# Two-block FFN groups with paired biases and a new order of issue in a sliding-window attention and highway FFN kernel

## The chip, the cores and the metric

The kernel runs on one core of one Trainium2 chip. The metric is the time of one execution on the device in microseconds (us). Before the change it is 175.66 us, the median of three runs (175.21 to 183.57). Executions fall into a fast and a slow state; in the slow one the granted clock of TensorE is mostly lower (0.961 in the slow run of the changed kernel, 0.971 to 0.982 in its fast ones).

Engines: PE is TensorE, PEld its weight loads, DVE is VectorE, ACT is ScalarE, POOL is GpSimd, SP is SyncE, which issues the stores.

## The reference, cut to what matters

```python
# attention: B = H = 8, S = 576, D = 64; a window of 128 keys, ALiBi bias
scores = scale * np.matmul(q, k.transpose(0, 1, 3, 2))
mask = (rel >= 0) & (rel < window)
scores = np.where(mask, scores + bias[None], -1000000000.0)
attn = softmax(scores)                    # written out in the original
x = attn @ v                              # rearranged to 4608 tokens x 512
# highway FFN
H = np.maximum(x @ w_h, 0.0)
T = 1.0 / (1.0 + np.exp(-(x @ w_t + b_t)))
out = T * H + (1.0 - T) * x
```

## The kernel before

Two batches go through the kernel as a pair, so there are four pairs. For each: GpSimd issues the loads (which cast to bf16), TensorE transposes Q and K, and computes scores; ScalarE takes the exponential, VectorE multiplies by the mask, TensorE multiplies by V, VectorE normalises into x. The FFN then works on blocks of 128 tokens, 36 in all:

```python
def f_h(m, kind, gi, i):                       # TensorE: H = x w_h, one PSUM bank
    AH[m, kind, gi] = ps_tile(1)
    for c in range(NCK):                       # NCK = 4
        nc.tensor.matmul(out=AH[m, kind, gi], lhsT=XT[m, kind, gi][:, i, c, :],
                         rhs=wH[:, c, :], start=c == 0, stop=c == NCK - 1)

def f_u(m, kind, gi):                          # VectorE: u = relu(H) - x
    ...
def f_z(m, kind, gi, i):                       # TensorE: Z = x w_t, then + b_t by a fifth matmul
    AZ[m, kind, gi] = ps_tile(1)
    az = AZ[m, kind, gi]
    for c in range(NCK):
        nc.tensor.matmul(out=az, lhsT=XT[m, kind, gi][:, i, c, :], rhs=wT[:, c, :],
                         start=c == 0, stop=False)
    nc.tensor.matmul(out=az, lhsT=ones1[:], rhs=bT[:], start=False, stop=True)

def f_th(m, kind, gi):                         # ScalarE: tanh(Z/2), float16
    ...
def f_t(m, kind, gi, eng):                     # GpSimd mostly: T = 0.5 tanh + 0.5
    tt = TT[m, kind, gi][:, 0 : grp(m, kind, gi)[1], :]
    eng.tensor_scalar(out=tt, in0=tt, scalar1=0.5, scalar2=0.5, op0=ALU.mult, op1=ALU.add)

def f_g(m, kind, gi):                          # VectorE: u = u T
    ...
def f_out(m, kind, gi, eng):                   # GpSimd mostly: out = u + x, float32
    bs, n, x = grp(m, kind, gi)
    ot = op.tile([P, 2, DM], F32, name="ot")
    OT[m, kind, gi] = ot
    eng.tensor_tensor(out=ot[:, 0:n, :], in0=UU.pop((m, kind, gi))[:, 0:n, :], in1=x, op=ALU.add)
```

`f_out` on GpSimd is "the sum" in what follows, `f_g` "the product", and the attention's multiplication by the mask "the mask". Each engine is given its instructions in a fixed order. The instructions are nodes of a graph, and a long list of numbers in the program, found by a search, gives the order in which they are issued; a second list gives each PSUM tile its bank:

```python
    names = list(nodes)
    ISSUE = """
        12 0 19 11 3 16 8 7 2 15 17 6 18 1 37 25 24 38 31 4 32 33 5 9 20 34 23 51 10 57 21 35 58
        ...                                    # 762 numbers in all
    """
```

The softmax here doesn't subtract the row's maximum and nothing guards it: scores larger than these inputs give would overflow.

## Time and profile before

| | before |
|---|---|
| time, median | 175.66 us |
| span of the profiled run | 173.5 us |
| busy: PE, DVE, ACT, POOL | 87, 81, 72, 68% |
| TensorE's last matmul ends | 166.2 us |
| from there to the end | 7.3 us |

These two groups, kept apart by form, give busy time and mean duration in ns, then idle time before them:

```profile
L364 DVE TENSOR_TENSOR pt<-pt,mk 128x2048 bf16<-128x2048 bf16 x24 | 34.7, 1454 | 0.8 <-ACT pt L345 0.8
...
L483 DVE TENSOR_TENSOR uu<-uu,tt 128x512 bf16<-128x512 bf16 x36 | 19.1, 538 | 4.3 <-POOL tt L478 4.1
```

A full mask takes 1.22 us in this trace when nothing holds it up, and 1.45 in the mean; a product 0.42, and 0.54 in the mean. Over the whole kernel these are 5.6 us (24 x 0.23) and 4.2 (36 x 0.12), and TensorE hardly notices: this is its list of waits of over 0.2 us for VectorE between 66 and 157 us (us in total, times, longest).

```profile
PE ps L329 <- DVE qt L290: 1.1, 1, 1.1
```

### The profile page before, as it was taken

To read this page: it belongs to the slowest core of one execution; us is meant where nothing else is said; L and a number is where in the kernel's file an instruction comes from. 1 tells how busy PE (TensorE), PEld (TensorE's weight loads), DVE (VectorE), ACT (ScalarE), POOL (GpSimd) and SP (SyncE) were. 2 spreads that over 40 slices of the span, in tenths; PEclk is the share of its full clock that TensorE was granted. 3 is DMA by queue.
4 is the path that set the end of the run, shared out by engine and by line. 5 is a ranking of instruction groups with operands and counts; after the bars stand their busy time and mean duration, and the time that the engine had idled before them with its cause. 6 is when DMAs were issued, how large, how long until landed. Compare 5 with 4: busy or idle time off the path is not lost.

```text
span 173.5 us, 5255 instructions
## 1 busy us (share of the span) xinstructions
PE 150.3 (87%) x2132; PEld 92.8 (54%) x2132; DVE 140.0 (81%) x244; ACT 125.4 (72%) x178; POOL 118.1 (68%) x132
## 2 busy tenths in 40 slices
PE   0169789999799789999999979999999999999930
PEld 0158544666566347766556755566556556754410
DVE  5087686999898888999867999889887899976580
ACT  2625678797799969899779968799898897235510
POOL 7997373488883799984067985884485969676540
PEclk9999999999999999999999999999999999999995
DMA  4999999999999999999999996793124332454443
GB/s 161 211 191 191 154 197 185 184 176 102 190 205 202 197 108 158 216 217 210 252 118 154 153 179 97 88 135 99 45 64 121 76 90 68 107 127 113 125 121 91
DMA packets 70167, 25.50 MB, mean 147 GB/s; under 512 B 48128, under 2 KB 65024, under 8 KB 70144
## 3 DMA queue, kind: packets, MB, share of 16 engines
q0 software_dynamic: 62832, 14.68, 120.7%
q1 hardware_dynamic: 7312, 10.49, 22.6%
q8 instruction: 16, 0.26, 0.7%
q14 instruction: 7, 0.06, 0.1%
HBM read 30.41 MB, written 9.44 MB: 230 GB/s over the span
## 4 chain that ended last, share of the span: by engine, by line
PE 53%; DMA 29%; DVE 5%; POOL 4%; ACT 3%; issue 2%; SPq 0%; POOLq 0%; ACTq 0%; DVEq 0%
DMA va<-in_v_dram 17%; PE ps L465 14%; PE ps L449 14%; DMA ktl<-in_k_dram 8%; PE ps L393 7%; PE ps L329 7%; PE ps L271 4%; PE ps L433 4%; DMA kl<-in_k_dram 3%; PE ps L467 3%; ACT pt L345 2%; DVE pt L364 1%; POOL kl L113 1%; DVE uu L456 1%; DMA out_dram<-ot 1%
## 5 line engine op out<-in xcount | busy, mean ns | idle before, releaser
L345 ACT ACTIVATE pt<-ps,bias 128x1024 bf16<-128x1024 f32 (+1 forms) x80 | 72.2, 950 | 13.5 <-PE ps L329 13.2
L489 POOL TENSOR_TENSOR ot<-uu,x 128x512 f32<-128x512 bf16 x35 | 47.7, 1365 | 24.9 <-DVE uu L483 24.8
L364 DVE TENSOR_TENSOR pt<-pt,mk 128x2048 bf16<-128x2048 bf16 (+1 forms) x40 | 46.5, 1174 | 0.8 <-ACT pt L345 0.8
L465 PE MATMUL ps<-wT,xt 128*128 128x512 bf16 x144 | 37.0, 379 | 1.0 <-DVE uu L456 0.8
L449 PE MATMUL ps<-wH,xt 128*128 128x512 bf16 x144 | 37.0, 386 | 0.3 <-DVE qt L290 0.3
L473 ACT ACTIVATE tt<-ps 128x512 f16<-128x512 f32 x36 | 21.6, 602 | 13.0 <-PE ps L467 11.9
L456 DVE SCALAR_TENSOR_TENSOR uu<-ps,x 128x512 bf16<-128x512 f32 x36 | 24.5, 684 | 4.6 <-PE ps L449 4.3
L329 PE MATMUL ps<-qt,kt 64*128 64x256 bf16 (+2 forms) x384 | 24.8, 248 | 3.4 <-DVE qt L290 1.1
L478 POOL TENSOR_SCALAR tt<-tt 128x512 f16<-128x512 f16 x32 | 21.8, 687 | 7.7 <-ACT tt L473 7.5
L410 DVE TENSOR_TENSOR x<-ps,rd 128x256 bf16<-128x256 f32 (+3 forms) x40 | 25.5, 638 | 1.4
L125 POOL DMA_DIRECT2D va<-in_v_dram x20 | 22.3, 1115 | 5.6 <-DMA ql<-in_q_dram 4.2
L393 PE MATMUL ps<-va,pt 128*128 128x65 bf16 (+1 forms) x576 | 24.9, 197 | 0.8 <-DMA va<-in_v_dram 0.7
L393 PEld LDWEIGHTS <-pt 128*128 128x128 bf16 (+1 forms) x576 | 21.1, 101 | 8.2 <-issue 2.9
L442 ACT COPY xt<-ps 128x512 bf16<-128x512 bf16 x36 | 20.7, 589 | 5.3 <-PE ps L433 5.1
L483 DVE TENSOR_TENSOR uu<-uu,tt 128x512 bf16<-128x512 bf16 x36 | 19.1, 538 | 4.3 <-POOL tt L478 4.1
L449 PEld LDWEIGHTS <-xt 128*128 128x128 bf16 x144 | 13.0, 99 | 14.3 <-issue 2.1
L465 PEld LDWEIGHTS <-xt 128*128 128x128 bf16 x144 | 12.9, 98 | 13.6 <-issue 1.5
L329 PEld LDWEIGHTS <-kt 64*128 64x128 bf16 x384 | 13.2, 96 | 12.9 <-issue 8.9
L271 PE MATMUL ps<-ident,kl 128*64 128x128 bf16 (+1 forms) x320 | 12.3, 228 | 8.1 <-DMA kl<-in_k_dram 7.9
L296 ACT COPY kt<-ps 128x1024 bf16<-128x1024 bf16 x13 | 13.0, 1020 | 5.4 <-PE ps L271 5.4
L271 PEld LDWEIGHTS <-kl 128*64 128x64 bf16 (+1 forms) x320 | 9.9, 126 | 10.1 <-DMA kl<-in_k_dram 8.4
L290 DVE COPY qt<-ps 128x1024 bf16<-128x1024 bf16 x16 | 11.0, 686 | 3.8 <-PE ps L271 3.7
(44 smaller groups left out, 125.5 us busy)
## 6 DMA issues: line engine op xcount, KB each, us to landing
out_dram<-ot SPq DMA_DIRECT2D x128, 64.0 KB, 2.4
va<-in_v_dram POOLq DMA_DIRECT2D x16, 256.0 KB, 14.2
ql<-in_q_dram POOLq DMA_DIRECT2D x3, 1024.0 KB, 16.0
kl<-in_k_dram POOLq DMA_DIRECT2D x3, 1024.0 KB, 15.7
ql<-in_moe_w_h_dram SPq DMA_DIRECT2D x1, 1024.0 KB, 5.2
out_dram<-ot SPq DMA_DIRECT2D x8, 128.0 KB, 2.4
kl<-in_k_dram POOLq DMA_DIRECT2D x4, 128.0 KB, 5.5
ql<-in_q_dram POOLq DMA_DIRECT2D x4, 128.0 KB, 5.9
```

What stands on the lines that cost most here:

```text
L125: nc.gpsimd.dma_start(out=VA[m % 2][0:n, c, :, :, 0:D].rearrange("s r h d -> s (r h) d"), in_=v[2 * m : 2 * m + 2, :, c * P : c * P + n, : ...
L271: nc.tensor.transpose(out=pt[r * D : (r + 1) * D, c : c + n], in_=L[ps, r, nh * hs + hl, t * D : (t + 1) * D], identity=ident[ps, ps],)
L329: nc.tensor.matmul(out=sc[:, r, o + off : o + off + w_], lhsT=KT[i][rows, h, j * P : (j + 1) * P], rhs=rhs, start=not add, stop=not add or ...
L345: nc.scalar.activation(out=PT[m, home, h // 2][:, h % 2, :, c0 : c0 + W], in_=SC[m, kind, h][:, :, o : o + W], func=ACTF.Exp, bias=BIAS[:, ...
L364: nc.vector.tensor_tensor(out=o, in0=o, in1=mk.to_broadcast([P, 2, rep, W]), op=ALU.mult,)
L393: nc.tensor.matmul(out=av[rows, hl, n * (D + 1) : (n + 1) * (D + 1)], lhsT=pt[:, hl, r, off : off + (D if narrow else P)], rhs=va[:, j, r, ...
L410: nc.vector.tensor_tensor(out=x.rearrange("p b (h d) -> p h b d", h=2), in0=av[:, :, :, 0:D], in1=rd[:, :, 0:nb].to_broadcast([P, 2, nb, D ...
L449: nc.tensor.matmul(out=AH[m, kind, gi], lhsT=XT[m, kind, gi][:, i, c, :], rhs=wH[:, c, :], start=c == 0, stop=c == NCK - 1)
L456: nc.vector.scalar_tensor_tensor(out=uu[:, 0:n, :], in0=AH[m, kind, gi].rearrange("p (i n) -> p i n", i=1), scalar=0.0, in1=x, op0=ALU.max ...
L465: nc.tensor.matmul(out=az, lhsT=XT[m, kind, gi][:, i, c, :], rhs=wT[:, c, :], start=c == 0, stop=False)
L478: eng.tensor_scalar(out=tt, in0=tt, scalar1=0.5, scalar2=0.5, op0=ALU.mult, op1=ALU.add)
L489: eng.tensor_tensor(out=ot[:, 0:n, :], in0=UU.pop((m, kind, gi))[:, 0:n, :], in1=x, op=ALU.add)
```

## The change

It puts the FFN's blocks into groups of two. Each group then needs one copy of x transposed, one evacuation of H, one tanh, one T, one product, one sum and half as many store issues. H and Z of a group take two PSUM banks each. The two bias matmuls of a group, which use one row of the array each, are put side by side into the upper and lower half of its rows, to run at the same time (the trace after will show 0.22 us for the two, as long as one took before). The order of issue and the list of banks come from a new search: this, too, is part of the change.

```diff
     GROUPS = {
-        "A": ((0,), (1,), (2,), (3,)), "B": ((0,), (1,), (2,), (3,), (4,)),
-        "a": ((0,), (1,)), "b": ((0,), (1,)), "c": ((0,), (1,)), "d": ((0,), (1,), (2,)),
+        "A": ((0, 1), (2, 3)), "B": ((0, 1), (2, 3), (4,)),
+        "a": ((0, 1),), "b": ((0, 1),), "c": ((0, 1),), "d": ((0, 1), (2,)),
     }
...
+        nc.vector.memset(hot2[:], 0.0)
+        for i in range(2):
+            nc.vector.memset(hot2[i * D : i * D + 1, :], 1.0)
...
-            nc.gpsimd.dma_start(out=bT[0:1, :], in_=moe_b_t.rearrange("(o n) -> o n", o=1))
+            for i in range(2):
+                nc.gpsimd.dma_start(
+                    out=bT[i * D : i * D + 1, :], in_=moe_b_t.rearrange("(o n) -> o n", o=1)
+                )
...
     def f_h(m, kind, gi, i):
-        AH[m, kind, gi] = ps_tile(1)
+        n = grp(m, kind, gi)[1]
+        if i == 0:
+            AH[m, kind, gi] = ps_tile(n).rearrange("p (i n) -> p i n", i=1) if n == 1 else ps_tile(n)
...
+    def f_zb(m, kind, gi):
+        AZ[m, kind, gi] = ps_tile(2)
+        for i in range(2):
+            rows = slice(i * D, (i + 1) * D)
+            nc.tensor.matmul(out=AZ[m, kind, gi][:, i, :], lhsT=hot2[rows, :], rhs=bT[rows, :],
+                             start=True, stop=False)
+
     def f_z(m, kind, gi, i):
-        AZ[m, kind, gi] = ps_tile(1)
-        az = AZ[m, kind, gi]
+        one = grp(m, kind, gi)[1] == 1
+        if one:
+            AZ[m, kind, gi] = ps_tile(1).rearrange("p (i n) -> p i n", i=1)
+        az = AZ[m, kind, gi][:, i, :]
         for c in range(NCK):
             nc.tensor.matmul(out=az, lhsT=XT[m, kind, gi][:, i, c, :], rhs=wT[:, c, :],
-                             start=c == 0, stop=False)
-        nc.tensor.matmul(out=az, lhsT=ones1[:], rhs=bT[:], start=False, stop=True)
+                             start=one and c == 0, stop=not one and c == NCK - 1)
+        if one:
+            nc.tensor.matmul(out=az, lhsT=ones1[:], rhs=bT[:], start=False, stop=True)
...
     ISSUE = """
-        12 0 19 11 3 16 8 7 2 15 17 6 18 1 37 25 24 38 31 4 32 33 5 9 20 34 23 51 10 57 21 35 58
+        14 0 16 3 7 2 18 6 11 12 17 1 19 31 25 5 32 35 24 8 36 33 212 15 34 37 29 51 38 57 52 4
...
```

Cut: the same widening in the other helpers (their formulas don't change), a separate entry for the groups of the last stage, which equals `B`, the graph's entries, and the rest of the two lists.

## The prediction

> **What bounds the kernel now.** I read the table of busy shares first, then the chain that ended last, then stretches of the timeline on TensorE, GpSimd and the store queue.
>
> ```profile
> PE 150.3 (87%) x2132; PEld 92.8 (54%) x2132; DVE 140.0 (81%) x244; ACT 125.4 (72%) x178; POOL 118.1 (68%) x132
> PE 53%; DMA 29%; DVE 5%; POOL 4%; ACT 3%; issue 2%; SPq 0%; POOLq 0%; ACTq 0%; DVEq 0%
> ```
>
> TensorE leads, but a busy share is an average, so I took the span in stretches:
>
> ```profile
> 24.00:46.00 22.00, 20.99 (x302) 13.09 (x299) 18.66 (x43) 17.34 (x29) 14.54 (x17) 1.00 2.29 164
> 46.00:151.00 105.00, 101.21 (x1456) 62.88 (x1457) 94.33 (x143) 88.92 (x115) 75.12 (x74) 1.00 1.46 142
> 151.00:166.30 15.30, 15.21 (x92) 7.32 (x91) 10.73 (x22) 6.29 (x11) 9.96 (x11) 1.00 0.47 117
> ```
>
> The first figure after the length is TensorE: 95, 96 and 99% busy from 24 us to its last matmul at 166.2 us. Before 24 us it waits for loads, and after 166.2 us come 7.3 us of tail. To see whether busy is work or waiting I priced TensorE's issue order from clean pieces of the chain:
>
> ```profile
> 66.63 0.60 PE ps L271 x16
> 107.61 0.22 PE ps L467
> 115.73 0.54 PE ps L329 x8
> 120.50 0.97 PE ps L449 x4
> 121.47 0.86 PE ps L465 x4
> 122.33 0.22 PE ps L467
> 122.55 0.22 PE ps L433 x4
> ```
>
> Four FFN matmuls take 0.86 us when the array's division stays and 0.97 us behind scores or V products of another division, so a change of division costs about 0.11 us. A bias matmul is 0.22, four transposes of x 0.22, one head's scores 0.215, sixteen transposes of Q or K 0.46, V products 0.26 to 0.9 by stage. Counting the issue order gives 135 changes of division (14.8 us) and 151.4 us of work. Laid against the trace, the first H matmul stands at 13.0 us of that tally and at 27.45 us in the trace (offset 14.4); the last matmul at 151.4 and 166.2 (offset 14.8). So after 27 us TensorE loses almost nothing, and its end is **work plus about 14.8 us lost at the start**. What delays the start is loads:
>
> ```profile
> 11.81 11.31 DMA va<-in_v_dram
> 26.31 17.49 DMA va<-in_v_dram
> 44.64 0.56 PE L393 MATMUL ps<-va,pt 128*128 128x65 bf16 x9
> 45.92 0.32 PE L393 MATMUL ps<-va,pt 128*64 128x65 bf16 x7 [0.73 <-DMA va<-in_v_dram]
> ```
>
> The second V block lands at 23.1 us, the fourth at 43.8, and V products wait 0.73 us for the fifth, until 45.9. The DMA engines are over 90% busy in nearly all of the first 100 us, so loads land in the order in which they are issued. These prices explain the 20.7 us between 23.1 and 43.8: 4.8 us for 1 MB of Q or K, 2.4 for the T weights or a 256 KB V block, 1.3 for a pair of 64 KB tails (three tails, weights, two big, two V: 3.9 + 2.4 + 9.6 + 4.8 = 20.7).
>
> **What the Trainium skill says.** "TensorEngine Tiling (Array Packing)", Key Properties: tiles run in parallel, but a change of tiling mode drains TensorE. The trace agrees: the 0.11 us above. "DMA: Bandwidth & Descriptors", Specifications: transfers want 512 B or more for line rate. It agrees: slices of the page in which mostly V and tails (128 B pieces) are in flight move 102 to 108 GB/s, those with Q and K about 200. "SBUF — State Buffer", Who interferes with whom: a VectorE instruction with two SBUF inputs and a GpSimd instruction that reads SBUF exclude each other, and so does VectorE's 2-port mode. It agrees:
>
> ```profile
> 61.19 1.15 POOL L489 TENSOR_TENSOR ot<-uu,x 128x512 f32<-128x512 bf16 x1
> 61.25 1.38 DVE L483 TENSOR_TENSOR uu<-uu,tt 128x512 bf16<-128x512 bf16 x1 [1.10 <-POOL tt L478]
> 105.30 3.31 DVE L364 TENSOR_TENSOR pt<-pt,mk 128x2048 bf16<-128x2048 bf16 x2
> 105.46 2.07 POOL L489 TENSOR_TENSOR ot<-uu,x 128x512 f32<-128x512 bf16 x1 [0.91 <-DVE uu L483]
> ```
>
> The product takes 0.42 us alone and 1.38 behind GpSimd's sum, and that sum 1.15 alone and 2.07 behind a mask. "ScalarE: Activation LUTs", Rules for kernel authors: about 0.3 us per instruction plus 0.83 ns per element. The trace decides otherwise: 0.602 us at 512 columns (tanh) and 1.119 at 1024 (exp), a fixed part near 0.085 us.
>
> **The change part by part.**
> 1. *Biases.* 36 bias matmuls become 16 pairs in the two row halves, plus 4 single ones: 20 times 0.216 us, not 36 times. Saved: 16 x 0.216 = 3.46 us, all on TensorE. A pair in row halves has the division of the scores: it is free of changes next to scores and costs two elsewhere. In the new order 10 of 16 pairs stand behind scores, one behind another pair, 5 behind something else; the changes are 136, against 135. TensorE's work: 151.4 - 3.46 + 0.11 = **148.0 us**.
> 2. *Two-block instructions.* 16 pairs of each. xt copy 2 x 0.589 - about 1.02: 2.5 us in all; tanh 2 x 0.602 - 1.12: 1.3 us; H evacuation 2 x 0.684 - about 1.22: 2.4 us; product 0.42 x 2 - about 0.69: 2.4 us. ScalarE and VectorE get lighter by 4 to 5 us each, beside TensorE: nothing directly. Stores fall from 136 to 72 issues, off the path until the end.
> 3. *Load order.* The new GpSimd order puts more ahead of the first batches' V. Before the fifth V block the old order issues the four small Q/K loads, two half loads, V 0 to 3, the T weights, Q and K of the next batches and two tails. The new one has all these and also two more tails and a V block of the next batches: 1.3 + 1.3 + 2.4 = 5.0 us. Landing: 45.9 + 5.0 = **50.9 us**. On the way the second V block comes behind 1 MB of K and three tails: 23.1 + 4.8 + 3.9 = 31.8 us.
>  TensorE needs that fifth block at tally 31.9 us in the new order; at the old offset it would be there at about 46.4 us. So it stalls some 4.5 us in several pieces. From there, remaining work is 148.0 - 31.9 = 116.1; the old kernel did a tally of 121.1 (from 30.3) in 120.3 us, so take 0.8 off: 50.9 + 115.3 = **166.2 us**, the old end of TensorE. The bias saving pays for the later load and no more.
> 4. *End.* The old tail:
>
> ```profile
> 166.25 1.15 POOL L489 TENSOR_TENSOR ot<-uu,x 128x512 f32<-128x512 bf16 x1 [0.74 <-DVE uu L483]
> 168.05 0.69 DVE L489 TENSOR_TENSOR ot<-uu,x 128x512 f32<-128x512 bf16 x1
> 169.25 1.11 SPq L497 DMA_DIRECT2D out_dram<-ot  x2
> ```
>
>  Its last store issue ends at 170.4, and the span 3.1 us later. In the new order the last two-block group ends only 1.9 us before TensorE does, and its store is issued after the single block's. With TensorE's end as zero: tanh of the pair ends at -0.7 (1.12 us), its T and product at about 1.2, GpSimd's two-block sum (estimate 2.2 us, from 1.15 for one) runs to 3.5. The last block's T and product use the port which that sum excludes them from: if the product loses, it ends at 4.0, the last sum at 4.7, its two store issues at 5.9, and four more (0.42 each) at 7.6. Plus 3.1: 10.7 us, against 7.3. If it wins, about 9. I take 10: **+2.7 us**.
>
> Sum of the chosen terms: -3.35 (biases and changes) + 4.0 (loads, 4.5 less the 0.5 to which the two tallies agree) + 2.7 (tail) = +3.35. I then allow 0.6 us back for lighter ScalarE and VectorE in the middle: 175.66 + 2.75 = **178.4 us**.
>
> **The rivals.**
> - *TensorE rules, loads are in time.* The bias saving counts whole, the tail costs 1.8 or so: 174 us. For it: 95 to 99% busy and the agreement of the tally. Against: the DMA engines are saturated early, so data cannot come sooner than its place in the queue.
> - *Banks.* H and Z of a group hold two of eight PSUM banks each for longer (estimate: per block 3.2 us of a bank instead of 1.8), and a group's T, product and sum form longer single waits. TensorE then idles in the middle too: 181 to 183 us. For it: the old order was fitted so closely that an in-order engine has no slack. Against: the old trace has hardly any wait for a bank, and the new order was searched with these costs.
> - *Longer exclusion between GpSimd and VectorE.* Two-block sums hold the port for 2.2 us. The total held time is the same, half as many collisions of twice the length, so VectorE (81%, soon less) should absorb it: no change.
>
> **Range and chances.** The landing is good to 1 us, the middle to 2, the tail to 1; together some 2.8 us of deviation. Range 174.8 to 182.0. Faster by over 2% needs under 172.1, more than the whole bias saving without any cost: 0.05. Slower by over 2% is above 179.2, just over my centre: 0.38. Within: 0.57.
>
> **What would show it.** Right: V products of the first batches waiting on the V load until about 51 us; TensorE's last matmul near 166; pair biases of about 0.22 us next to scores; a tail of 9 to 11 us with the two-block sum on GpSimd in it. Wrong: the last matmul near 162 (loads were in time), or above 169 with waits on ScalarE, VectorE or GpSimd between 60 and 150 us (banks and buffers), or a tail that stays at 7 us.

## More of the kernel before

TensorE is the busiest engine, and the prediction shows that it is busy nearly all the time from 24 us to its end. The lines that it doesn't show concern VectorE. These are the stretches of the later middle; the columns are the stretch, its length, then busy time and number of instructions of PE, PEld, DVE, ACT and POOL, granted clock, share of the DMA engines and GB/s.

```profile
90.00:110.00 20.00, 18.87 (x274) 11.78 (x273) 18.83 (x27) 17.40 (x23) 15.64 (x16) 1.00 1.89 142
110.00:130.00 20.00, 19.77 (x256) 11.95 (x255) 17.64 (x28) 17.56 (x24) 13.80 (x13) 1.00 0.64 82
130.00:150.00 20.00, 19.61 (x244) 11.91 (x242) 17.86 (x28) 15.94 (x23) 14.68 (x14) 1.00 0.36 93
```

VectorE, the third figure, is busy for 88 to 94% of them: it has little room.

## The result, and the profile after

The changed kernel takes 184.95 us in the median of four runs, beside 175.44 for the kernel before in the same rounds; the ratio of the fast runs is 1.052 [1.037, 1.067]. The second submission gives 184.59 beside 175.19, ratio 1.0549 [1.0485, 1.0614]. A ratio is the mean time of one kernel's fast runs over that of the other's from the same rounds, so it isn't quite the ratio of the medians. The kernel is slower by some 9.5 us. The prediction said 178.4 and at most 182.0: it was wrong, and in the rival that it thought to cost nothing.

The busy shares and the chain that ended last, from the page of the changed kernel (span 182.7 us):

```profile
PE 148.6 (81%) x2108; PEld 92.0 (50%) x2132; DVE 142.7 (78%) x213; ACT 122.5 (67%) x146; POOL 110.6 (61%) x103
...
DVE 27%; PE 24%; DMA 20%; issue 10%; POOL 9%; ACT 5%; SPq 1%; POOLq 0%; DVEq 0%; ACTq 0%
```

Two things are to be seen. VectorE has gone from 5% of the chain to 27, TensorE from 53 to 24: what ends last is now often VectorE. And VectorE's busy time has *risen*, from 140.0 to 142.7 us, although the two-block instructions save it about 5 us of work. ScalarE and GpSimd did get lighter. So VectorE's instructions have become longer:

```profile
L373 DVE TENSOR_TENSOR pt<-pt,mk 128x2048 bf16<-128x2048 bf16 x24 | 39.9, 1682 | 1.7 <-ACT pt L354 1.6
...
L509 DVE TENSOR_TENSOR uu<-uu,tt 128x1024 bf16<-128x1024 bf16 x16 | 12.7, 801 | 1.9 <-POOL tt L504 1.9
```

The 24 full masks are what they were, and yet take 1.68 us in the mean, against 1.45 before. What holds them up can be seen in the timeline (start, length, engine, line; in brackets the idle time before it; what it waits for inside itself isn't marked):

```profile
101.99 3.85 DVE L373 TENSOR_TENSOR pt<-pt,mk 128x2048 bf16<-128x2048 bf16 x1 [0.55 <-ACT pt L354]
...
102.60 2.15 POOL L515 TENSOR_TENSOR ot<-uu,x 128x1024 f32<-128x1024 bf16 x1
...
105.77 0.68 DVE L471 SCALAR_TENSOR_TENSOR uu<-ps,x 128x512 bf16<-128x512 f32 x1
```

The sum ends at 104.75 us, the mask at 105.84: the mask did its 1.1 us of work after the sum, and VectorE's next instruction, which empties PSUM for TensorE, waited with it. (The mask's first 0.6 us lie ahead of this sum, beside loads that GpSimd was issuing. I don't explain them: other masks beside such issues take 1.22 us.) The stretches show what this leaves of VectorE's room:

```profile
90.00:110.00 20.00, 18.55 (x226) 10.54 (x228) 18.26 (x19) 17.18 (x19) 15.63 (x12) 1.00 2.50 154
110.00:130.00 20.00, 18.11 (x272) 11.68 (x274) 18.36 (x25) 16.30 (x18) 9.50 (x8) 1.00 0.68 75
130.00:150.00 20.00, 18.73 (x228) 11.27 (x230) 19.44 (x20) 15.59 (x16) 12.57 (x7) 1.00 0.29 77
```

VectorE is at 91, 92 and 97%, and from 110 to 150 us TensorE is busy for 36.8 us, where it was for 39.4 (some 4 of its 504 matmuls there are missing from the trace, some 0.9 us at 0.22 each). Its waits between 66 and 157 us, in the same form as before:

```profile
PE ps L402 <- DVE pt L373: 1.6, 2, 1.2
PE ps L280 <- DMA kl<-in_k_dram: 1.4, 1, 1.4
PE ps L402 <- DVE x L419: 1.3, 2, 1.1
PE ps L338 <- DVE uu L471: 1.1, 3, 0.7
```

With the smaller ones, which I leave out, these are 5.7 us for VectorE and 1.8 for loads, against 1.1 and none. Only the first line waits for data, a masked tile. In all the others for VectorE, 4.1 us, TensorE doesn't need what VectorE writes (V products don't read x, scores don't read u): it waits for a PSUM bank that VectorE has not emptied yet. The chain of waits shows one such place, and the bias pair beside it (start, length, what):

```profile
116.01 2.69 DVE pt L373
...
118.86 0.84 DVE x L419
...
119.74 0.40 PE ps L338 x8
...
121.44 0.22 PE ps L481 x2
```

A mask of 2.69 us, then a normalisation (`x`), which frees a bank; then TensorE may go on with scores (L338). The pair of biases at 121.44 costs 0.22 us for two, next to scores: this part works as it was meant to.

The tail, from the timeline:

```profile
171.59 0.38 PE L493 MATMUL ps<-bT,ones 128*128 128x512 bf16 x1
...
173.24 2.12 POOL L515 TENSOR_TENSOR ot<-uu,x 128x1024 f32<-128x1024 bf16 x1 [1.14 <-DVE uu L509]
173.34 2.29 DVE L509 TENSOR_TENSOR uu<-uu,tt 128x512 bf16<-128x512 bf16 x1
175.67 0.69 DVE L515 TENSOR_TENSOR ot<-uu,x 128x512 f32<-128x512 bf16 x1
...
177.60 1.95 SPq L531 DMA_DIRECT2D out_dram<-ot  x4
```

The last product of one block needs 0.42 us and takes 2.29, behind the two-block sum. From TensorE's end at 172.0 to the end of the span are 10.7 us.

The whole difference can now be split with the prediction's own means: the tally of TensorE's work, what TensorE has lost by its end (its end less the tally), and the tail. I give all later kernels in this table as well. The tally prices the order of issue, with 0.11 us for each change of the array's division; it is my working, the other columns are from the profiles.

| kernel | tally (changes) | TensorE's end | lost by then | tail | span |
|---|---|---|---|---|---|
| before | 151.4 (135) | 166.2 | 14.8 | 7.3 | 173.5 |
| changed | 148.0 (136) | 172.0 | 23.9 | 10.7 | 182.7 |
| changed, sums as two memsets | 148.0 (136) | 165.4 | 17.3 | 9.0 | 174.4 |
| two-block groups, order B | 145.8 (116) | 162.0 | 16.1 | 9.5 | 171.5 |
| the same, sums as two memsets | 145.8 (116) | 161.3 | 15.4 | 7.3 | 168.6 |
| single blocks, first new order, repeated | 148.6 (110) | 163.3 | 14.6 | 7.5 | 170.8 |

Before to changed: -3.4 of work, +9.1 lost, +3.4 of tail, which is the 9.2 us between the spans up to rounding. Followed along the trace, the loss before the middle is 18.1 us at 66.4 us (it was 16.0 at 60.8 before), 21.1 at 105, 23.2 at 156 and 23.9 at the end. After these two points the changed kernel loses 5.8 us more, while the kernel before got 1.2 back: 7.0 of the 9.1 us arise there, and 2.1 ahead of it.

### The profile page after: what moved, and what is told of

The parts are those of the page before. It is cut to its first block, busy times and chain, and to the rows that moved or that the text cites.

```text
span 185.6 us, 5020 instructions
## 1 busy us (share of the span) xinstructions
PE 153.0 (82%) x2132; PEld 92.9 (50%) x2132; DVE 142.9 (77%) x213; ACT 122.3 (66%) x146; POOL 110.7 (60%) x103
## 4 chain that ended last, share of the span: by engine, by line
PE 33%; DVE 30%; DMA 21%; issue 6%; ACT 6%; POOL 1%; DVEq 0%; ACTq 0%; POOLq 0%
DVE pt L373 13%; DMA kl<-in_k_dram 12%; PE ps L464 9%; DMA ql<-in_q_dram 8%; PE ps L490 7%; PE ps L402 6%; PE ps L338 6%; DVE uu L471 5%; ACT pt L354 5%; DVE uu L509 4%; DVE x L419 3%; PE ps L280 3%; DVE qt L299 2%; DVE rd L418 1%; PE ps L481 1%
## 5 line engine op out<-in xcount | busy, mean ns | idle before, releaser
L373 DVE TENSOR_TENSOR pt<-pt,mk 128x2048 bf16<-128x2048 bf16 (+1 forms) x40 | 52.9, 1341 | 2.6 <-ACT pt L354 2.5
L515 POOL TENSOR_TENSOR ot<-uu,x 128x1024 f32<-128x1024 bf16 (+1 forms) x19 | 41.4, 2180 | 20.9 <-DVE uu L509 20.1
L504 POOL TENSOR_SCALAR tt<-tt 128x1024 f16<-128x1024 f16 (+1 forms) x18 | 19.7, 1096 | 32.8 <-ACT tt L499 32.8
L338 PE MATMUL ps<-qt,kt 64*128 64x256 bf16 (+2 forms) x384 | 27.1, 254 | 4.8 <-DVE qt L299 1.6
L471 DVE SCALAR_TENSOR_TENSOR uu<-ps,x 128x1024 bf16<-128x1024 f32 (+1 forms) x20 | 22.2, 1110 | 8.4 <-PE ps L464 7.4
L499 ACT ACTIVATE tt<-ps 128x1024 f16<-128x1024 f32 (+1 forms) x20 | 18.8, 941 | 11.7 <-PE ps L490 10.0
L455 ACT COPY xt<-ps 128x1024 bf16<-128x1024 bf16 (+1 forms) x20 | 18.4, 935 | 5.2 <-PE ps L445 5.2
L338 PEld LDWEIGHTS <-kt 64*128 64x128 bf16 x384 | 14.4, 97 | 14.3 <-issue 10.3
L280 PE MATMUL ps<-ident,ql 128*64 128x128 bf16 (+1 forms) x320 | 11.5, 228 | 10.0 <-DMA ql<-in_q_dram 9.7
L509 DVE TENSOR_TENSOR uu<-uu,tt 128x1024 bf16<-128x1024 bf16 (+1 forms) x20 | 15.7, 795 | 2.0 <-POOL tt L504 1.9
L418 DVE RECIPROCAL rd<-ps 128x4 f32<-128x4 f32 (+3 forms) x40 | 7.9, 197 | 11.8 <-PE ps L402 10.3
L299 DVE COPY qt<-ps 128x1024 bf16<-128x1024 bf16 x16 | 10.7, 684 | 6.1 <-PE ps L280 6.1
```

The lines of the kernel that those rows point to most:

```text
L338: nc.tensor.matmul(out=sc[:, r, o + off : o + off + w_], lhsT=KT[i][rows, h, j * P : (j + 1) * P], rhs=rhs, start=not add, stop=not add or ...
L373: nc.vector.tensor_tensor(out=o, in0=o, in1=mk.to_broadcast([P, 2, rep, W]), op=ALU.mult,)
L471: nc.vector.scalar_tensor_tensor(out=uu[:, 0:n, :], in0=AH[m, kind, gi], scalar=0.0, in1=x, op0=ALU.max, op1=ALU.subtract,)
L509: nc.vector.tensor_tensor(out=uu, in0=uu, in1=TT.pop((m, kind, gi))[:, 0:n, :], op=ALU.mult)
```

## The experiments

My theory after the result: in the new order VectorE is on the critical path from about 66 us on, and the exclusion between GpSimd's sums and VectorE's masks and products is what makes it late. By exclusion I mean that an instruction of one engine stands still while one of the other runs. Rivals: two-block instructions are at fault as such (longer waits for banks and tiles); late loads; the bias pairs; the tail alone. Each diff is against the changed kernel unless it says otherwise. A run's gain is told by its ratio, times 175.2 us; the brackets are 95% intervals, and of two runs whose intervals overlap the smaller differences are not clear of noise.

**The changed kernel again.** No edit. It serves the others as their base.

> The changed kernel once more, unedited, to get a profile in its fast state (the one of the result fell in its slow state, 187.3 us, with the granted clock at 0.87 to 0.92 in three stretches). All theories: 1.04 to 1.06 times the time of before. If the lost time is work of the order and of waits (theory: VectorE held up by longer GpSimd instructions, TensorE waiting behind it), the fast profile still has VectorE in 25 to 30% of the chain of waits and masks of 2 to 4 us each; if the low clock was the cause, the fast profile shows TensorE ending before 170 us and masks near 1.2 us.

Measured: 184.59 us, ratio 1.0549 [1.0485, 1.0614], profile in the fast state. The result is real, and a slow clock has no part in it.

**Biases apart.** The two biases of a group as two full-height matmuls.

```diff
         for i in range(2):
-            rows = slice(i * D, (i + 1) * D)
-            nc.tensor.matmul(out=AZ[m, kind, gi][:, i, :], lhsT=hot2[rows, :], rhs=bT[rows, :],
+            nc.tensor.matmul(out=AZ[m, kind, gi][:, i, :], lhsT=ones1[:], rhs=bT[:],
                              start=True, stop=False)
```

> Row-half pairs undone alone: the two biases of a group are two full-array matmuls at the same place of the order. If TensorE's work sets the time (my prediction), it costs 16 x 0.216 us less the 10 changes of division that go with the pairs not behind scores (5 x 0.22 us), some +2.4 us against the changed kernel (ratio to before about 1.065). If TensorE waits for VectorE anyway (rival), it costs under 1 us, because the extra matmuls fill waits.

Measured: 186.82 us, ratio 1.0691 [1.0610, 1.0772], so 2.5 us slower than with the pairs, on intervals that just overlap. The bias part of the change saves time and isn't the cause. The expected 2.4 rests on a miscount: by the order of issue, undoing the pairs removes 4 changes of division (136 become 132), not 10, so TensorE's work rises by 3.46 - 0.44 = 3.0 us.

**The final sum one block at a time.** Two GpSimd instructions of one block each in place of one of two, so that VectorE can get in between.

```diff
-        eng.tensor_tensor(out=ot[:, 0:n, :], in0=UU.pop((m, kind, gi))[:, 0:n, :], in1=x, op=ALU.add)
+        uu = UU.pop((m, kind, gi))
+        for i in range(n):
+            eng.tensor_tensor(out=ot[:, i, :], in0=uu[:, i, :], in1=x[:, i, :], op=ALU.add)
```

> Only the final sum u+x is issued per block (two GpSimd instructions of about 1.15 us instead of one of 2.1 us); order and everything else as in the changed kernel. Theory (VectorE's masks wait out the long sums under the port's exclusion): the wait of a mask is at most about 1.1 us instead of 2.1, masks' mean falls from 1.34 towards 1.2 us, the kernel gains 2 to 5 us. Rival (load order and the in-order sequence cost the time): under 1 us either way.

Measured: 182.77 us, ratio 1.0463 [1.0396, 1.0529]: 1.5 us of the 9.5, by overlapping intervals. VectorE's busy time falls from 142.7 to 138.3 us and the full masks to 1.43 us in the mean, as before the change (the 1.34 of the expectation is a mean of full and half masks). The direction is right, but the width of the sum is only a small part. How small isn't well measured: the profiled run, the slowest of the four, also waits 3.3 us for a load of Q, which the changed kernel's profile doesn't.

**All elementwise FFN instructions one block at a time.** The copy of x, the evacuation, tanh, T, product and sum, each in the way of the edit before; the order of issue stays.

> All elementwise instructions of a group (x copies, H evacuation, tanh, T, product, sum) are issued per block again; groups, banks, bias pairs and order of issue stay. Theory of the exclusion: like the split sum or better, minus some 2.2 us of fixed cost on VectorE and 4 us on ScalarE: 0 to 5 us faster than the changed kernel. Rival that the order of issue alone costs the time: within 1.5 us of the changed kernel. Rival that two-block instructions are what saves time: 3 to 5 us slower.

Measured: 183.59 us, ratio 1.0495 [1.0414, 1.0576]: 1 us better, not clear of noise, with the masks still at 1.60 us. Two-block instructions as such are not the cause. (That a group holds two banks for each of H and Z stays as it is here; the control and order B below speak to that.) Short instructions in the new order are nearly as slow, so the order itself must be looked at.

**The last two-block sum on VectorE**, ahead of the last T, and its store first.

```diff
-                end = last and gi == len(groups(m, kind)) - 1
+                end = last and gi
```

> The sum of the last two-block group goes to VectorE (as that of the last block has been), ahead of the last block's T, and its store is issued first. In the changed kernel TensorE ends at 172.0 us and the span at 182.7: 10.7 us. Theory (the two-block sum on GpSimd shuts VectorE out of the last product for 2.1 us, then six store issues follow): the rest after TensorE falls to about 8 us, the kernel gains 2 to 3 us. Rival (the end is set by the store's landing whatever runs before): under 1 us.

Measured: 183.59 us, ratio 1.0492 [1.0439, 1.0545]: 1 us better, by overlapping intervals. In its profile 8.7 us follow TensorE's end, not 10.7; a clock of 0.89 from 150 to 165 us makes the span itself a poor guide. The tail is a part of the loss: 2 us of it by this trace, 1 us by the times, which noise could also make.

**K of the last pair loaded before Q.** Its wait was TensorE's longest for a load in the middle (1.4 us). The two big loads change places, and a transpose is moved behind them.

> Loads of the last pair: K goes into the queue where Q went, three V blocks and one Q earlier, Q where K went; the first transposes of that Q move to just ahead of their copy. In the changed kernel TensorE waits 1.45 us for K at 85.4 us and is only 87% busy from 70 to 90 us, and VectorE 71%. Theory (late loads there cost the time and make VectorE catch up later): the wait for K goes, 2 to 4 us gained. Rival (the time is lost between VectorE and TensorE later, whatever the loads): under 1 us.

Measured: 184.54 us, ratio 1.0524 [1.0465, 1.0582]: nothing beyond the noise. The wait for K is gone, and another has come in its place (TensorE's waits from 60 to 110 us):

```profile
PE ps L445 <- DVE qt L299: 1.8, 2, 1.5
```

It was 0.7 us in the changed kernel. By 105 us TensorE is where it was to 0.2 us. TensorE's wait for a load in this stretch was free: without it, VectorE held TensorE up instead.

**The sums as a memset, in the changed kernel.** GpSimd writes the output tile without reading anything. Its output is wrong, which doesn't matter for the time.

```diff
-        eng.tensor_tensor(out=ot[:, 0:n, :], in0=UU.pop((m, kind, gi))[:, 0:n, :], in1=x, op=ALU.add)
+        if eng is nc.vector:
+            eng.tensor_tensor(out=ot[:, 0:n, :], in0=UU.pop((m, kind, gi))[:, 0:n, :], in1=x, op=ALU.add)
+        else:
+            UU.pop((m, kind, gi))
+            eng.memset(ot[:, 0:n, :], 1.0)
```

> Wrong result on purpose: the sums on GpSimd write a constant and read nothing from SBUF, so they can't shut VectorE out; all the rest as in the changed kernel. Shows the whole price of the exclusion by sums, and of the sums' length. If it is what makes the changed kernel slow: masks at 1.22 us each, 5 us or more gained (below 178 us). If the order of issue is: 1 to 3 us, and it stays above 180 us.

Measured: 175.76 us, ratio 1.0022 [0.9966, 1.0078]: 9 us faster, nearly the whole loss.

**The same in the kernel before.**

> The same in the kernel before (wrong result on purpose). If exclusion by one-block sums costs it as much as two-block sums cost the other: gain as large as in the changed kernel (1 to 5 us). If short sums fit into its waits: under 1 us, as its TensorE is 96 to 99% busy anyway.

Measured: 174.06 us, ratio 0.997 [0.991, 1.003]: 0.5 us, not clear of noise, and at most 1.6 by the interval. So the same exclusion that costs the changed kernel 9 us costs the kernel before next to nothing, though VectorE's busy time falls by 9.8 us here, too (140.0 to 130.2). Both kernels lose VectorE's time to it, and only in one is that time on the path.

**The sums as two memsets**, a control. One memset is also shorter than the sum (0.95 us against 2.12), which could by itself free tiles earlier.

```diff
-            eng.memset(ot[:, 0:n, :], 1.0)
+            for val in (0.5, 1.0):
+                eng.memset(ot[:, 0:n, :], val)
```

> Wrong on purpose, a control for the run whose GpSimd sums were replaced by one memset: here each is two memsets one after the other, some 1.9 us for a two-block group (2 times the 0.95 us that one memset took), so that GpSimd is as busy and the output tiles come free as late as with the real sums (2.12 us), but it reads nothing. Theory (VectorE is held up by the sums' reads and writes): the time stays at 175 to 177.5 us, as with one memset (175.8). Rival (the sum's length is what costs, by late output tiles, late stores and a late T on GpSimd): 181 to 185 us.

Measured: 176.56 us, ratio 1.0043 [0.9952, 1.0134]: the length of the sums costs nothing measurable. TensorE has no idle time in the stretch where it lost most:

```profile
90.00:110.00 20.00, 20.00 (x248) 11.42 (x247) 14.62 (x22) 17.70 (x19) 10.37 (x12) 1.00 2.03 156
```

VectorE is busy for 14.62 us of these 20, where it was for 18.26; over the span it is 128.6 us, 14 less than in the changed kernel. This is its group of full masks:

```profile
L373 DVE TENSOR_TENSOR pt<-pt,mk 128x2048 bf16<-128x2048 bf16 x24 | 29.3, 1239 | 2.4 <-ACT pt L354 2.3
```

They take 1.24 us in the mean beside memsets, so a GpSimd instruction that only writes doesn't hold them up. TensorE's waits for VectorE between 66 and 157 us are down from 5.7 to 0.8 us, with the same groups in the same banks. One thing the control does not keep: a memset needn't wait for the product, a sum must. It therefore also frees GpSimd a little earlier, and the end of the kernel: of the 8.3 us between the two spans, 6.6 are TensorE's and 1.7 the tail's. In the body that can hardly matter, since GpSimd wasn't late in the changed kernel: of the 17 records of its T there, 16 begin within 0.1 us of the end of their tanh, and the K load that TensorE waits for was issued at 62.5 us there and at 63.8 in the control.

The control also shows where the loads come in. Both kernels issue in the same order, so I can compare them at the same bias pair. At the third recorded pair the control is 1.3 us *behind* (58.89 us after 57.59), at the last 6.6 ahead (157.26 after 163.87). What it loses first is this:

```profile
50.87 0.32 PE L402 MATMUL ps<-va,pt 128*64 128x65 bf16 x7 [1.97 <-DMA va<-in_v_dram]
```

It waits for the fifth V block, until the very time that the prediction gave (50.9). The changed kernel, held up by VectorE, comes to these products only at 50.3 us, and doesn't wait.

These runs settle that the exclusion is the cost, but not whether it comes with two-block groups or with the order that they were given. For that I made orders of my own, by a search that prices each instruction as the traces do and lets VectorE's masks and products and GpSimd's sums and T wait for each other. Only the two lists of numbers differ, so there is no diff to show; some four fifths of all instructions move by more than five places.

**Two-block groups, a first new order.**

> The changed kernel's own instructions, two-block groups and paired biases, in an order that I searched myself: each instruction has the mean duration that the two traces show for it when it is not held up, and VectorE's products and masks and GpSimd's sums and T wait for each other. Theory (the grouping is sound, it is the placing of its wide instructions under exclusion that loses; TensorE has 3.4 us less to do): at or under the kernel before, 170 to 176 us. Rival (wide instructions lose in any order, since one that waits holds two blocks): 179 us or more. The search's own figure for this order is 13 to 15 us under its figure for the changed kernel, which is an estimate; I expect two thirds of it.

Measured: 181.64 us, ratio 1.0282 [1.0186, 1.0378], or 180 us by its two fast runs. The figure is the rival's, but not for the rival's reason: the masks are down to 1.36 us in the mean, while TensorE waits for loads of Q that my search had landing up to 9 us too early. (The profile is of a slow run, so its waits only show where to look.)

```profile
PE ps L280 <- DMA ql<-in_q_dram: 11.8, 4, 7.2
```

7.2 us of this is the start of the kernel; the rest is new. This order decides nothing about the grouping.

**Single blocks, a first new order.** The kernel before with its two lists replaced.

> The kernel before, ungrouped, its instructions unchanged, in an order from the same search of mine with the same exclusion. If a search that knows of the exclusion is what brings time, and not the grouping, this one gains as much: 168 to 173 us, and stands level with the two-block kernel in its new order. If grouping is itself worth the 3.4 us of TensorE's work, this one is 2 to 4 us behind the two-block kernel in its new order. If the order of the kernel before was already at what it can reach, 174 to 177 us.

Measured: 172.74 us, ratio 0.9826 [0.9752, 0.9901]: 3 us faster than the kernel before. So the kernel before was not at its best order either.

**Two-block groups, order B and order C**, from a search that takes loads to be up to 20% slower.

> The changed kernel's instructions in a second order of my own, searched with the exclusion between VectorE and GpSimd in it, and with loads taken up to 20% slower than in the trace so that it doesn't lean on them. If the order was at fault and not the grouping: 170 to 176 us, with VectorE's full masks back at 1.2 to 1.4 us in the mean (1.68 in the changed kernel). If wide sums lose in any order: 179 us or more, as the first one (181.6), with no long wait for a load this time.

Measured for B: 174.27 us (14 runs), ratio 0.9932 [0.9906, 0.9959]. Ten microseconds faster than the changed kernel, with exactly the same instructions. By the table, of the 11.2 us between the two spans 2.2 are fewer changes of division (116 after 136), 7.8 are time that TensorE no longer loses, and 1.2 are tail. This is its page, and its full masks by form:

```profile
PE 145.1 (85%) x2111; PEld 93.0 (54%) x2132; DVE 129.5 (76%) x213; ACT 122.4 (71%) x146; POOL 111.4 (65%) x103
...
PE 53%; DVE 17%; POOL 7%; issue 6%; DMA 6%; ACT 6%; POOLq 1%; DVEq 0%; ACTq 0%
```

```profile
L373 DVE TENSOR_TENSOR pt<-pt,mk 128x2048 bf16<-128x2048 bf16 x24 | 31.9, 1339 | 0.4 <-ACT pt L354 0.4
```

VectorE's busy time is 13 us less than in the changed kernel, for the same instructions; the masks are at 1.34 us, and TensorE has the chain again. GpSimd's sums are as wide and as many as ever (2.18 us in the mean in both). They only stand elsewhere.

> As the run before it, from another start of the same search, so that one unlucky order isn't taken for the grouping's worth: 170 to 176 us if the order was at fault, 179 or more if the grouping is; if the two of them lie more than 3 us apart, the search's figures say nothing at this grain.

Measured for C: 184.25 us, ratio 1.0519 [1.0472, 1.0565]. From the same search, and 10 us slower, with masks at 1.53 us and waits of TensorE of 3.1 and 2.8 us for VectorE. Taken alone it would speak for the grouping as the fault, but my expectation's last sentence applies: the search's own figures don't tell orders apart at this grain, and only the chip does. The 10 us are not a clean figure, either: all four runs of C have a granted clock of 0.947 to 0.959, where the runs of B have 0.972 to 0.988. In C's profile it is 0.83 from 60 to 80 us and 0.91 from 100 to 120, and no run here tells whether that is C's own waits or the state of the chip. The comparison of B with the changed kernel (0.969 to 0.982) is free of this.

**Single blocks, a second new order**, from the search with late loads.

> The kernel before, ungrouped, from this same search with late loads. If grouping brings its 3.4 us of TensorE's work in a fair order, this one is 2 to 3 us slower than the better of the two two-block orders, at 172 to 176 us. If the grouping brings nothing or costs something even so, this one is level with them or faster, like the first single order (172.7).

Measured: 182.46 us (179.65 to 183.36), all against my expectation. Three of the four runs and the profile are slow, and no ratio of fast runs came out, so I use it only to say that single blocks, too, can be ordered badly: the one fast run took 179.65 us.

**Order B with the sums as two memsets** (wrong).

> Wrong on purpose: pairs_b with GpSimd's final sums as two memsets, as the control run had it in the changed kernel, where it saved 8 us. If pairs_b is 10 us better than the changed kernel because its sums stand where VectorE has time to wait, there is little left to save: 172 to 174.3 us, 0 to 2 us under pairs_b. If it is better for another reason, such as loads, and exclusion costs it as much as the changed kernel, it falls to 165 to 168 us.

Measured: 170.53 us, ratio 0.9732 [0.9675, 0.9788]: 3.5 us faster than order B, more than the 0 to 2 expected and less than half of what it was in the changed kernel. The table splits it: TensorE's loss falls by 0.7 us and the tail by 2.2. In order B the last product is followed by a two-block sum of 2.11 us, which the memset need not follow; that is a wait for data and no exclusion. In the body, exclusion by the sums costs order B 0.7 us, where it cost the changed order 6.6.

**Order B with the biases apart.**

> pairs_b with the paired biases undone, two full-height bias matmuls for each group. If this order is bound by TensorE (93 to 99% busy from 25 us on in its trace) the price is again the work, +2.4 us as in the changed kernel: 176.3 to 177 us. If another engine sets its pace, less than 1 us.

Measured: 175.74 us, ratio 1.0036 [1.0000, 1.0073], so 1.8 us slower than order B. Less than the 2.4 expected, more than the 1 of the rival. The 2.4 was taken over from the changed order; counted in this one, undoing the pairs leaves the number of changes as it is, so TensorE's work rises by the whole 3.46 us. About half of it shows: TensorE sets part of this order's pace, not all.

**The first order of single blocks, repeated** beside the two runs above, on one chip.

> The first ungrouped order once more, for a comparison on one chip. If its 0.983 of the kernel before is real: 0.978 to 0.988 again, 171.5 to 173.5 us, so 1 us faster than pairs_b (0.993). If the first was luck of four runs: within 0.5% of pairs_b.

Measured: 172.98 us, ratio 0.9783 [0.9710, 0.9856]. The gain over the kernel before is real, near 2% (three of the six runs are slow), and this is the fastest correct kernel. Its tally says where most of it is from: 110 changes of the array's division against 135, at 0.11 us each, is 2.75 us less work for TensorE. That is argued from the tally, not shown by a run of its own.

What stays open: whether two-block groups are better or worse than single blocks at their best. The best orders that I found lie 2.6 us apart in favour of single blocks (0.9783 after 0.9932, on intervals that don't overlap), while orders of the same two-block instructions differ by 10 us; so the 3.4 us that the bias pairs save cannot be credited or denied to the change as a whole.

## Why the prediction was right or wrong, point by point

1. *Biases: right.* It priced the pairs at 3.35 us of TensorE's work. Undoing them costs 2.5 us in the changed kernel, where the work rises by 3.0, and 1.8 in order B, where it rises by 3.5; a pair beside scores takes 0.22 us in the trace. The rule that a pair away from scores costs two changes is too high: it costs two, one or none by what stands on its two sides.
2. *Two-block instructions: the step that failed.* It said that ScalarE and VectorE get lighter by 4 to 5 us each, "beside TensorE: nothing directly", and allowed 0.6 us back in the middle. ScalarE did get lighter, by 2.9 us of busy time, with a two-block tanh of 1.03 us, not 1.12. (The 1.12 was an exp's.) VectorE did not: 142.7 us busy after 140.0. From 66 us on the kernel didn't gain 0.6 us on the one before but lost 7.0.
3. *Load order: the right mechanism, half the size, and hidden.* The fifth V block was to land at 50.9 us, 5.0 later than before. In the changed kernel it was issued at 34.1 us and took 14.4, so it landed at 48.5, 2.6 later, and TensorE has no wait for it. What TensorE does wait for between 25 and 66 us is VectorE, three times, 1.0 us in all. The loss ahead of 66 us is 2.1 us above that of before, where the prediction had 4.0 for the loads. In the control, with the same order of loads, the block took 16.5 us, landed at 50.8, and TensorE waited 2.0 us for it: of the 2.5 us that the control still loses more than the kernel before, these are most.
4. *End: right, in its parts too.* It took 10 us, and gave 10.7 for the case in which the last product loses against the two-block sum. It lost, and the tail is 10.7 us.

The rival that came true is the third, "longer exclusion between GpSimd and VectorE", of which the prediction said: same total time held, half as many collisions of twice the length, VectorE at 81% "should absorb it: no change". Two errors lie in this. First, VectorE's 81% is an average over the span; in the stretches from 90 to 150 us it was already at 88 to 94%, and what cannot be absorbed there is lost. The prediction's own line from 46 to 151 us has VectorE at 94.33 of 105 us, 90%, but it read only TensorE there. Second, it assumed that the collisions stay as many as the sums. What counts is how much of VectorE's wait falls where TensorE needs the result soon, and that is the order's doing: with the same instructions the exclusion costs TensorE 6.6 us in the changed order and 0.7 in order B, and about 0.5 us of time, not clear of noise, in the kernel before.

The sum, as it was and as it came out: biases -3.35 (work -3.4), loads +4.0 (+2.1, all that was lost ahead of 66 us), tail +2.7 (+3.4), middle -0.6 (+7.0, of which the control takes back 6.6). Middle and loads are TensorE's 9.1 us, and 1.7 of the tail go with the sums, too. The prediction's test, "above 169 with waits on ScalarE, VectorE or GpSimd between 60 and 150 us", is what the trace showed, for VectorE alone. It had put that down to banks, and so far it was right: 4.1 of the 5.7 us are waits for a bank. But the groups' hold on the banks is not the cause, as the rival *Banks* (181 to 183 us) had it: the control has the same groups and banks, and 0.8 us of such waits. The banks are late because VectorE is.

## What to carry to other kernels

Take every engine in stretches, not only the busiest: an engine at 81% over the span may have no room where the change adds to it. When VectorE and GpSimd both read operands in SBUF, as here, add up how much longer VectorE's instructions are than their clean length, and replace GpSimd's instruction by a memset to learn what the exclusion costs; a change that lengthens GpSimd's instructions needs its order checked on the chip for where they stand. And judge a change that comes with a new order only against other orders of both versions, since here the order alone was worth 10 us, while the best orders found for the two versions lie 2.6 us apart.

## What the Trainium skill lacked or had wrong

- "SBUF — State Buffer", Who interferes with whom: its rules hold here (masks beside memsets that only write stay at 1.24 us; behind two-block sums they reach 3.85). What it lacks is the size of it in a kernel: it cost 9 us of 184.6 in one kernel and at most 1.6 of 175 in another, so the rule alone can't tell whether a kernel is hurt.
- "TensorEngine Tiling (Array Packing)", Key Properties: says that a change of mode drains TensorE, but gives no figure. Here it is about 0.11 us, and the kernels have from 110 to 136 of them, 12 to 15 us of TensorE's work.
- No page: how far two orders of the same instructions can lie apart. By fast runs, two-block groups took 174, 180, 184 (at a lower clock) and 185 us, single blocks 171 to 172, 175 and, in one run, 180.
